# Issuing the q, k and v loads of a local-attention and feed-forward kernel from GpSimd instead of SyncE

## The chip, the cores and the metric

The kernel runs on one core of one Trainium2 chip. The metric is the device time of one execution in microseconds (us). A core has five engines with an instruction queue each: TensorE (PE, matrix products, with a weight load of its own, PEld), VectorE (DVE), ScalarE (ACT), GpSimd (POOL) and SyncE (SP), which here only issues transfers. Every engine takes its instructions in order, and a transfer (DMA) is an instruction in the queue of the engine that issues it: it waits there until its inputs and its buffer are ready, and what stands behind it waits too. The profile counts the transfers that GpSimd issues as one queue (q0, software_dynamic) and those that SyncE issues as another (q1, hardware_dynamic); both are carried out by the same 16 DMA engines.

## The reference

Local attention in chunks of 64 tokens, then a feed-forward layer with a leaky rectifier, all in float32:

```python
# q, k, v: (8 batches, 8 heads, 576 tokens, 64), cut to chunks of 64 tokens
scores = matmul(q_c, k_c.T) / 8 - max
attn   = exp(scores) / (sum(exp(scores)) + 1e-9)
out    = matmul(attn, v_c)                  # (4608 tokens, 512)
h      = out @ w_in                         # 512 -> 2048
result = (max(h, 0) + alpha * min(h, 0)) @ w_out   # 2048 -> 512
```

## The kernel before

The 4608 tokens are 36 sub-blocks of 128 tokens (two chunks, eight heads) and 9 blocks of 512 tokens. The first three blocks go through the feed-forward layer plainly: each of its products is done as three products of float32r halves (high by high, high by low, low by high). The other six blocks go in three pairs, with products of combined quarters (seven in place of eight); the quarters of the weights are computed in the first part on VectorE (`combine`, L607), written to DRAM by GpSimd (`keep_a`, L591) and streamed back through a ring of four buffers of 512 KB (`stream`, L643, issued by GpSimd too, L654).

The attention of the first eight sub-blocks is at the start, in an order written out by hand. Each of the other 28 (numbers 8 to 35) has a *visit* between two stretches of feed-forward products: 14 visits in the plain part, 14 in the first products of the first two pairs. At the visit of sub-block s (`visit_scores`, L512) TensorE does the value product of sub-block s-2 (L388) and the scores of s (L272). Then the loads of q and k of sub-block s+2 and of v of sub-block s are traced (`attn_load`, L232). A load has to wait for its buffer: q and k for the scores just done (two buffers each), v for the value product just done. The softmax of s follows on VectorE and ScalarE; VectorE transposes its result in blocks of 32 by 32 (L331), and eight transfers of 32 KB each (`attn_blocks`, L338) put the blocks in their places in the tile `pT`, from which the value product of s two visits later reads. So each visit has eleven transfers: three loads of 256 KB and eight of `pT`.

Other transfers that matter below: two sums of block 0 and 1 with an earlier part in DRAM are added by GpSimd's transfers (`partial<-g`, L499, and L636); the buffer `g` that the first of them reads is also the one that ScalarE fills with the negative part of the next hidden block (L406), which VectorE completes (L409). The results that were summed in DRAM are copied to the output by SyncE near the end of the plain part (`finals`, L957).

A planner orders each engine's queue from a simulated time line and from priorities; visits have a high priority. TensorE is kept in the order of tracing from the 21st step on. `tc.issue_after(ins)` puts instructions behind `ins` in its engine's queue. The hand-written start is not touched.

Of the kernel before, what the change touches and what calls it, by code (L numbers as in the profile page):

```python
# [59 lines left out]
def tile_local_attention_prelu_ffn(  # L60
# [12 lines left out]
    nc = tc.nc  # L73
    P = 128
    NSUB, C = qT.shape[1], 64
# [14 lines left out]
    EARLY = 2 * SPB  # L90
# [20 lines left out]
    def f32(t):  # L111
        return t.bitcast(F32)
# [103 lines left out]
    def prepare(f, behind=None):  # L216
        with tc.issue_after(behind.ins) if behind else nullcontext():
            for side in ("wi", "wo"):
                fetch(side, f)
                for _ in piece(side, f):  # L220
                    pass
# [2 lines left out]
    att = []  # L224

    qkv = {}
    loads = []
    probs = {}
    stages = {}
    pdiag = {}  # L230

    def attn_load(s, parts="qkv"):  # L232
        if "q" in parts:
            q_sb, kb = (load.tile([P, H, C], F32, name=name, bufs=2) for name in ("q_sb", "k_sb"))
            for t, src in ((q_sb, qT), (kb, kT)):
                nc.sync.dma_start(out=t, in_=src[:, s].rearrange("p (h t) -> p h t", t=C))
            qkv[s] = [q_sb, kb, None]
        if "v" in parts:
            v_sb = load.tile([P, DM], F32, name="v_sb", bufs=2)
            loads.append(nc.sync.dma_start(out=v_sb, in_=v[:, s]))  # L240
            qkv[s][2] = v_sb

    def banks_of(token):
# [83 lines left out]
    def attn_blocks(s):  # L327

        pr = probs.pop(s)
        tb = stage.tile([P, 2, H, HALF], F32, name="t3", bufs=2)  # L330
        nc.vector.transpose(tb.rearrange("p j h t -> p h j t"), pr)  # L331
        pT = load.tile([P, 2, H, HALF], F32, name="pT", bufs=2)
        for c in range(2):
            for i in range(2):
                for j in range(2):
                    src = slice(c * C + i * HALF, c * C + (i + 1) * HALF)
                    dst = slice(c * C + j * HALF, c * C + (j + 1) * HALF)
                    nc.sync.dma_start(  # L338
                        out=pT[dst, i].rearrange("p h t -> p (h t)"),
                        in_=tb[src, j].rearrange("p h t -> p (h t)"),  # L340
                    )
        pdiag[s] = pT
# [161 lines left out]
    def new_x():  # L504
        return (xp.tile([P, NK, TB], F32R, name="xh"), xp.tile([P, NK, TB], F32R, name="xl"))
# [22 lines left out]
    def visit_results(old, xo, new, sc3):  # L528
        if old is not None:
            attn_x(old, xo)  # L530
        if new is not None:
            attn_blocks(new)

    def visit(old, new):
        with tc.high_priority(offset=HIGH):
            parts = visit_scores(old, new)
            visit_softmax(*parts)
            visit_results(*parts)
# [9 lines left out]
    def first_v(s):  # L548

        v_sb = (vs + vs2)[s // 2].rearrange("p s h t -> p s (h t)")  # L550
        loads.append(nc.sync.dma_start(out=v_sb, in_=v[:, s:s + 2]))
        for i in range(2):
            qkv.setdefault(s + i, [None] * 3)[2] = v_sb[:, i]

# [42 lines left out]
    def keep_quarters(f):  # L597

        j, second = f % JF, f >= JF
        keep_a("wi", 4 if second else 1, j, wi[f][:, :, halves[second]])  # L600
        keep_a("wo", 4 if second else 1, j, wo[f][:, :, halves[second]])
        if second:
            keep_a("wo", 2, j, wo[f][:, :, halves[0]])
        else:
            keep_a("wi", 2, j, wi[f][:, :, halves[1]])

    def combine(side, j, early):  # L607

        ws = wi if side == "wi" else wo
        pair = [ws[j], ws[JF + j]]  # L610
        left, right = halves
        a = []
        for w, name in zip(pair, ("ta", "tb")):
            t = stage.tile([P, 512], F32, name=name, bufs=1)
            nc.vector.tensor_tensor(t, f32(w[:, 0]), f32(w[:, 1]), op=ALU.add)
            a.append(t)
        a11, a22 = a[0][:, left], a[1][:, right]
        if side == "wi":
            a12, a21 = a[0][:, right], a[1][:, left]
        else:  # L620
            a21, a12 = a[0][:, right], a[1][:, left]
        nc.vector.tensor_tensor(a22, a21, a22, op=ALU.add)
        nc.vector.tensor_tensor(a21, a11, a21, op=ALU.subtract)
        nc.vector.tensor_tensor(a11, a22, a11, op=ALU.subtract)
        nc.vector.tensor_tensor(a12, a12, a11, op=ALU.subtract)
        names = ((2, 4), (3, 1)) if side == "wi" else ((2, 3), (4, 1))
        for t, name, which in zip(a, names, ("raw", "raw" if early else "more")):
            w = scratch(which, [P, 2, 512], F32R)
            nc.scalar.copy(w[:, 0], t)
            nc.vector.tensor_tensor(w[:, 1], t, f32(w[:, 0]), op=ALU.subtract)  # L630
            for half, s in zip((left, right), name):
                stored = keep_a(side, {1: 5, 2: 6, 3: 7, 4: 3}[s], j, w[:, :, half])
            if adds:
                to, what = adds.pop(0)
                with tc.issue_after(stored.ins):
                    nc.gpsimd.dma_start(out=to, in_=what, accum_op=ALU.add)  # L636
# [231 lines left out]
    def new_raw(b):  # L868
        for n, name in enumerate(("xh", "xl")):
            x[b + n] = xp.tile([P, NK, TB], F32, name=name)  # L870
# [67 lines left out]
    for n, (p, b, f) in enumerate(steps):  # L938
        _, f0, f1 = phases[p]
        if f == f0:  # L940
            acc = accs[b] if p == 1 else []
            if p >= 3 and b + 1 < PLAIN:
                x[b + 1] = new_x()
        if n == 2 * NF:
            new_raw(PLAIN)
        if n == n0 + 1:

            tick = nc.gpsimd.tensor_copy(out=table, in_=f32(x[1][1])[:, 0, TB - 1:])
        if n0 < n <= n0 + NF:
            with tc.issue_after(tick.ins):  # L950
                keep_quarters(n - n0 - 1)
        pinned[0] = n >= 20
        if n == len(steps) - 1:
            with tc.issue_after(loads[-1].ins):
                while finals:
                    dst, src = finals.pop(0)
                    nc.sync.dma_start(out=dst, in_=src)  # L957
        if n < begun:
            continue
        if 2 * n in late:  # L960
            if 2 * n == visits[0]:
                with tc.issue_after(listed.ins):
                    for ahead in range(2):
                        attn_load(EARLY + ahead, "q")
            visit(*late[2 * n])
            parts, entry = held
            with tc.high_priority(offset=HIGH), tc.issue_after(stages["softmax"][0].ins):
                with tc.issue_after(stages["stored"].ins):
                    *_, entry[1] = parts
        if ready < NF:  # L970
            for ready in range(ready, min(n + 2, NF)):
                prepare(ready, split_ends.get(("wo", ready - 1)) if n == begun else None)
            ready += 1
        elif n in COMBINE:

            with tc.issue_after(stages["softmax"][0].ins), tc.issue_after(stages["softmax"][1].ins):
                combine(*combined.pop(0), n in (29, 35))
        if n == len(steps) - 8:
            ops, conversion = convert(PLAIN)
        if len(steps) - 8 <= n < len(steps) - 4:  # L980
            conversion.pop(0)()
        parts = first_layer(x[b], f)
        next(parts)
        entry = [acc, None, f, f0, f1, b, False]
        pending.append(entry)
        waits = 2 * n + 2 in late and n + 1 < len(steps)
        with tc.high_priority(offset=HIGH):
            next(parts)
            if not waits:
                next(parts)  # L990
        if 2 * n + 1 in late:
            visit(*late[2 * n + 1])
        if waits:
            held = parts, entry
        else:
            with tc.high_priority(offset=HIGH), (
                tc.issue_after(stages["softmax"][0].ins) if 2 * n + 1 in late else nullcontext()
            ):
                *_, entry[1] = parts
        if n >= len(steps) - 3:  # L1000

            with tc.issue_after(stages["split"][0].ins):
                for _ in range(3):
                    conversion.pop(0)()

        if len(pending) > (1 if n < 20 else 2):
            second(*pending.pop(0))
# [68 lines left out]
```

## Time and profile before

| | |
|---|---|
| median of 3 runs | 773.77 us (773.28 to 774.55) |
| the profiled execution's own time | 774.44 us |
| its span, first to last instruction | 772.6 us |
| TensorE busy | 760.5 us, 98% |
| VectorE, ScalarE, GpSimd busy | 84%, 58%, 24% |
| granted TensorE clock | 1.00 of full speed throughout |

Times inside the span are counted from its first instruction. The plain part lasts to about 304 us, the first pair to 464, the second to 621, the third to the end. Busy TensorE is not by itself TensorE at its peak; between large products the starts of neighbouring matrix products of 512 columns are 0.22 us apart where nothing holds them up.

### The profile page before, as it was taken

To read this page: it belongs to the slowest core of one execution; us is meant where nothing else is said; L and a number is where in the kernel's file an instruction comes from. 1 tells how busy PE (TensorE), PEld (TensorE's weight loads), DVE (VectorE), ACT (ScalarE), POOL (GpSimd) and SP (SyncE) were. 2 spreads that over 40 slices of the span, in tenths; PEclk is the share of its full clock that TensorE was granted. 3 is DMA by queue.
4 is the path that set the end of the run, shared out by engine and by line. 5 is a ranking of instruction groups with operands and counts; after the bars stand their busy time and mean duration, and the time that the engine had idled before them with its cause. 6 is when DMAs were issued, how large, how long until landed. Compare 5 with 4: busy or idle time off the path is not lost.

```text
span 772.6 us, 15413 instructions
## 1 busy us (share of the span) xinstructions
PE 760.5 (98%) x5558; PEld 639.8 (83%) x5558; DVE 647.7 (84%) x1140; ACT 448.2 (58%) x1221; POOL 184.8 (24%) x304
## 2 busy tenths in 40 slices
PE   7999999999999999999999999999999999999998
PEld 6788888878888888888888888888888888888886
DVE  6999989997979976877899898777898977679784
ACT  6975555566665674665756446654574544354642
POOL 1153322442525320111112111111121122112110
PEclk9999999999999999999999999999999999999999
DMA  9859496566969685888775678876556776655674
GB/s 359 325 194 385 175 329 210 174 237 179 285 206 260 231 302 168 293 283 273 258 246 200 229 248 280 273 236 209 204 203 219 253 233 193 202 205 193 199 242 158
DMA packets 69322, 184.52 MB, mean 239 GB/s; under 512 B 10992, under 2 KB 18176, under 8 KB 69120
## 3 DMA queue, kind: packets, MB, share of 16 engines
q0 software_dynamic: 34336, 119.56, 46.4%
q1 hardware_dynamic: 34480, 63.20, 24.2%
q8 instruction: 44, 0.72, 0.4%
q10 hardware_dynamic: 432, 0.79, 0.3%
q14 instruction: 30, 0.25, 0.1%
HBM read 135.27 MB, written 42.99 MB: 231 GB/s over the span
## 4 chain that ended last, share of the span: by engine, by line
PE 77%; DMA 6%; DVE 5%; ACT 5%; SPq 5%; issue 1%; POOL 0%; DVEq 0%; ACTq 0%
PE ps_o L717 19%; PE ps_o L845 19%; PE ps_h L717 10%; PE ps_h L845 10%; PE ps_h L421 7%; SPq L338 4%; PE ps_oa L457 4%; PE ps_ob L457 4%; DMA raw<-w_in 2%; DMA pT<-t 2%; PE ps_a L388 2%; ACT wi L313 1%; PE ps_a L272 1%; ACT wo L313 1%; DMA partial<-g 1%
## 5 line engine op out<-in xcount | busy, mean ns | idle before, releaser
L421 PE MATMUL ps_h<-xh,wi 128*128 128x512 f32 x384 | 101.7, 385 | 0.7 <-DVE g L409 0.5
L421 PEld LDWEIGHTS ps_h<-xh,wi 128*128 128x128 f32 x384 | 70.8, 187 | 13.8 <-PE ps_ob L457 0.8
L717 PE MATMUL ps_o<-wi,raw 128*128 128x512 f32 x336 | 79.1, 382 | 0.0
L717 PEld LDWEIGHTS ps_o<-wi,raw 128*128 128x128 f32 x336 | 62.5, 187 | 11.2
L673 ACT CAST gh<-wo 128x512 fp32r<-128x512 f32 x66 | 41.0, 621 | 47.3 <-PE ps_o L845 31.7
L287 ACT ACTIVATE pr<-ps_a,mx 128x64 f32<-128x64 f32 x224 | 67.4, 326 | 0.8
L457 PE MATMUL ps_oa<-wo,gh 128*128 128x512 f32 x192 | 58.4, 384 | 0.0
L457 PE MATMUL ps_ob<-wo,gh 128*128 128x512 f32 x192 | 57.7, 380 | 0.0
L421 PE MATMUL ps_h<-xl,wi 128*128 128x512 f32 x192 | 50.6, 381 | 0.0
L674 DVE TENSOR_TENSOR gl<-wo,gh 128x512 fp32r<-128x512 f32 x63 | 43.3, 687 | 7.5 <-ACT gh L673 7.1
L287 ACT ACTIVATION_READ_ACCUMULATOR pr<-ps_a,mx 128x1 f32 x224 | 48.7, 217 | 0.0
L654 POOL DMA_DIRECT2D raw<-wi_a x42 | 22.4, 533 | 96.1 <-PE ps_o L717 54.1
L654 POOL DMA_DIRECT2D raw<-wo_a x42 | 22.3, 531 | 90.7 <-PE ps_o L845 50.9
L406 ACT ACTIVATE wo<-gh 128x512 f32<-128x512 f32 x24 | 15.2, 633 | 48.4 <-DVE gh L747 48.4
L673 ACT CAST ta<-wo 128x512 fp32r<-128x512 f32 x42 | 26.1, 621 | 26.6 <-PE ps_o L845 15.5
L421 PEld LDWEIGHTS ps_h<-xl,wi 128*128 128x128 f32 x192 | 35.8, 187 | 6.8 <-DVE xl L375 0.3
L457 PEld LDWEIGHTS ps_ob<-wo,gh 128*128 128x128 f32 x192 | 35.9, 187 | 6.4
L457 PEld LDWEIGHTS ps_oa<-wo,gh 128*128 128x128 f32 x192 | 35.4, 187 | 6.6 <-DVE xl L375 0.2
L717 PE MATMUL ps_o<-wi,wo 128*128 128x512 f32 x168 | 40.4, 383 | 0.0
L717 PE MATMUL ps_o<-wi,wi 128*128 128x512 f32 x168 | 40.4, 383 | 0.0
L717 PE MATMUL ps_h<-wi,raw 128*128 128x512 f32 x168 | 40.4, 382 | 0.0
L435 ACT CAST gh<-g 128x512 fp32r<-128x512 f32 x48 | 30.2, 630 | 16.9 <-DVE g L409 15.0
(296 smaller groups left out, 2036.1 us busy)
## 6 DMA issues: line engine op xcount, KB each, us to landing
raw<-wi_a POOLq DMA_DIRECT2D x42, 512.0 KB, 4.5
raw<-wo_a POOLq DMA_DIRECT2D x42, 512.0 KB, 4.4
wi<-wi_a POOLq DMA_DIRECT2D x21, 512.0 KB, 4.4
wo<-wi_a POOLq DMA_DIRECT2D x21, 512.0 KB, 4.6
wi<-wo_a POOLq DMA_DIRECT2D x21, 512.0 KB, 4.2
wo<-wo_a POOLq DMA_DIRECT2D x21, 512.0 KB, 4.4
k_sb<-kT SPq DMA_DIRECT2D x28, 256.0 KB, 4.2
q_sb<-qT SPq DMA_DIRECT2D x28, 256.0 KB, 3.9
```

The lines of the kernel that those rows point to most:

```text
L287: last = nc.scalar.activation(pr[:, g], sc3[:, g // NP, g % NP], AF.Exp, bias=mx[:, g], scale=SCALE, accum_out=sm[:, g])
L313: last = nc.scalar.activation(pr[:, g], sc3[:, g % 2, g // 2], AF.Exp, bias=mx[:, g], scale=SCALE, accum_out=sm[:, g])
L338: nc.sync.dma_start(out=pT[dst, i].rearrange("p h t -> p (h t)"), in_=tb[src, j].rearrange("p h t -> p (h t)"),)
L388: pe(nc.tensor.matmul(att[0][par * C:(par + 1) * C, c, hp * C:(hp + 1) * C], lhsT=v_sb[rows, h * C:(h + 1) * C], rhs=p[rows, :, par * NP + ...
L421: pe(nc.tensor.matmul(woven(hps), lhsT=wi[f][:, l, k * P:(k + 1) * P], rhs=woven(xx[:, k]), start=(i == 0 and k == 0), stop=(i == 2 and k ...
L435: nc.scalar.copy(gh, g)
L457: pe(nc.tensor.matmul(woven(o), lhsT=a[:, ts], rhs=woven(wo[f][:, l]), start=(f == first and i == 0), stop=(f == last and i == 2),))
L654: streamed[0] = nc.gpsimd.dma_start(out=f32(t), in_=units[side][n])
L673: hi = nc.scalar.copy(t_hi, t)
L674: return hi, nc.vector.tensor_tensor(t_lo, t, f32(t_hi), op=ALU.subtract)
L717: pe(nc.tensor.matmul(woven(ps), lhsT=w[:, l, k * P:(k + 1) * P], rhs=woven(xx[:, xl]), start=first and at == 0, stop=at == n - 1, skip_gr ...
L845: pe(nc.tensor.matmul(woven(ps[m]), lhsT=w[:, l, m * P:(m + 1) * P], rhs=woven(xx), start=i in (1, 5, 2) and j == 0 and n == 0, stop=j == ...
```

## The change

The loads of sub-blocks 8 and 9 stay on SyncE; from sub-block 10 on (26 sub-blocks, 78 loads) they are issued by GpSimd. SyncE keeps the `pT` transfers and the stores. The `finals`, which were put behind the latest load of v, are put behind the latest `pT` transfer, since both must be on SyncE.

```diff
-    loads = []
     def attn_load(s, parts="qkv"):
+        queue = nc.sync if s < EARLY + 2 else nc.gpsimd
         if "q" in parts:
             ...
             for t, src in ((q_sb, qT), (kb, kT)):
-                nc.sync.dma_start(out=t, in_=src[:, s].rearrange("p (h t) -> p h t", t=C))
+                queue.dma_start(out=t, in_=src[:, s].rearrange("p (h t) -> p h t", t=C))
         if "v" in parts:
             v_sb = load.tile([P, DM], F32, name="v_sb", bufs=2)
-            loads.append(nc.sync.dma_start(out=v_sb, in_=v[:, s]))
+            queue.dma_start(out=v_sb, in_=v[:, s])
...
-                    nc.sync.dma_start(
+                    stages["blocks"] = nc.sync.dma_start(
                         out=pT[dst, i].rearrange("p h t -> p (h t)"),
...
-        loads.append(nc.sync.dma_start(out=v_sb, in_=v[:, s:s + 2]))
+        nc.sync.dma_start(out=v_sb, in_=v[:, s:s + 2])
...
-            with tc.issue_after(loads[-1].ins):
+            with tc.issue_after(stages["blocks"].ins):
```

## Rows read from the trace of the kernel before

**Rows 1.** The page, part 1: busy time and share of the span, instructions.
```profile
PE 760.5 (98%) x5558; PEld 639.8 (83%) x5558; DVE 647.7 (84%) x1140; ACT 448.2 (58%) x1221; POOL 184.8 (24%) x304
```

**Rows 2.** Busy time by stretch: length; busy (instructions) by engine; clock, DMA share, GB/s.
```profile
150.00:200.00 50.00, 49.25 (x455) 40.83 (x454) 44.99 (x91) 33.12 (x122) 17.49 (x23) 1.00 0.71 213
200.00:250.00 50.00, 49.15 (x512) 40.84 (x512) 44.05 (x86) 29.38 (x105) 22.25 (x29) 1.00 0.84 248
...
700.00:750.00 50.00, 50.00 (x229) 42.49 (x228) 40.76 (x66) 25.31 (x44) 10.10 (x19) 1.00 0.66 212
```

**Rows 3.** Waits of PE: line and releaser; total us, times, longest.
```profile
PE ps_a L388 <- DMA pT<-t: 1.1, 3, 0.4
```

**Rows 4.** PE in order of time, at visits: start us, us, instruction, count, idle before.
```profile
159.67 0.69 PE L388 MATMUL ps_a<-pT,v_sb 64*64 64x64 f32 x32
...
160.76 1.17 PE L421 MATMUL ps_h<-xh,wi 128*128 128x512 f32 x4
...
181.51 0.33 PE L388 MATMUL ps_a<-pT,v_sb 64*64 64x64 f32 x2
...
183.22 0.71 PE L457 MATMUL ps_oa<-wo,gh 128*128 128x512 f32 x2
...
191.35 0.69 PE L388 MATMUL ps_a<-pT,v_sb 64*64 64x64 f32 x32
...
212.45 0.33 PE L388 MATMUL ps_a<-pT,v_sb 64*64 64x64 f32 x2
...
214.28 0.71 PE L457 MATMUL ps_oa<-wo,gh 128*128 128x512 f32 x2
```

**Rows 5.** SP's queue in order of time.
```profile
173.97 5.68 SPq L338 DMA_DIRECT2D pT<-t  x8
...
183.47 5.64 SPq L338 DMA_DIRECT2D pT<-t  x8
...
199.61 0.53 SPq L236 DMA_DIRECT2D q_sb<-qT  x1
...
201.18 7.87 SPq L338 DMA_DIRECT2D pT<-t  x8
...
221.97 4.95 SPq L338 DMA_DIRECT2D pT<-t  x8
```

**Rows 6.** DVE in order of time.
```profile
182.08 0.75 DVE L409 SCALAR_TENSOR_TENSOR g<-g,rise,ps_h 128x512 f32<-128x512 f32 x1 [1.90 <-ACT g L406]
182.74 0.70 DVE L331 STREAM_TRANSPOSE t<-pr 128x512 f32<-128x512 f32 x1
...
199.85 0.70 DVE L331 STREAM_TRANSPOSE t<-pr 128x512 f32<-128x512 f32 x1
```

**Rows 7.** POOL in order of time, plain part.
```profile
174.47 1.45 POOL L593 DMA_DIRECT2D wi_a<-raw  x2
175.92 0.98 POOL L499 DMA_DIRECT2D partial<-g  x1
191.58 1.47 POOL L593 DMA_DIRECT2D wi_a<-raw  x2 [14.67 <-DVE raw L630]
```

**Rows 8.** ACT in order of time, around the wait for that sum.
```profile
174.64 0.62 ACT L491 COPY g<-ps_ob 128x512 f32<-128x512 f32 x1
...
181.45 0.60 ACT L406 ACTIVATE g<-ps_h 128x512 f32<-128x512 f32 x1 [2.56 <-DMA partial<-g]
```

**Rows 9.** Line L957, the finals: duration ns min/median/max, first and last start.
```profile
L957 SPq DMA_DIRECT2D out<-partial x8: 533/539/560, 284.8 to 294.3; - x8
```

**Rows 10.** POOL in order of time, first pair: streams.
```profile
326.70 0.53 POOL L654 DMA_DIRECT2D wi<-wi_a  x1 [2.11 <-PE ps_h L717]
...
335.93 0.53 POOL L654 DMA_DIRECT2D raw<-wi_a  x1 [2.11 <-PE ps_o L717]
```

**Rows 11.** Line L654, the streams: duration of an issue (ns), and time to landing.
```profile
L654 POOL DMA_DIRECT2D raw<-wi_a x42: 531/531/572, 274.0 to 679.7; - x42
...
DMA to landing us min/median/max: 3.4/4.5/6.5
```

## The prediction

> **What bounds the kernel now.** I read the page's busy times first. TensorE is busy for 98% of the span [rows 1], so whatever the change does, it shows only where it makes TensorE stand or lets it go on. Busy is not peak, so I next read TensorE's stretches and the starts of its products. Between 250 and 750 us each of the ten stretches of 50 us is busy to within 0.02 us, the last of them shown, and the large products start 0.22 us apart throughout. Idle time away from the two ends lies in two stretches: 0.75 us in 150 to 200 and 0.85 us in 200 to 250 [rows 2]. The granted clock is 1.00 in all of them, the upper of its two levels, and nothing in the change bears on it. The waits name the cause for most of it: the value product of a visit waits for transposed blocks, 1.1 us in three places [rows 3].
>
> What such a wait costs is more than its idle time. An undisturbed visit takes 160.76 - 159.67 = 1.09 us from its first small product to the next large one. The visit at 181.51 took 1.71, so it lost 0.62; the one at 212.45 took 1.83 and lost 0.74 [rows 4]. The third in the list I count like the second, which makes about 2.1 us in all. That is the most the change can give back: 0.27%. A difference of up to 0.2% (1.55 us) is what a measurement of this kernel can hardly tell from none, so only a nearly complete cure would be seen. There is much more room on the other side.
>
> **What leaves SyncE.** 78 of its issues. Per visit the three loads held SP's queue from 199.61 to 201.18, 1.57 us [rows 5]. Whether that matters depends on what stands behind. For the visit at 212.45 it does: the transposes on VectorE ended at 199.85 + 0.70 = 200.55, the `pT` group could begin only at 201.18 [rows 5, 6]. Beginning at once gives 0.63 us of the 0.74 lost; I take the part beyond the queue's usual lag of 0.05 us: **-0.58 us**. For the visit at 181.51 SP was free when the group began at 173.97, and the group took 5.68 us; TensorE needed its last piece 7.5 us after its start [rows 4, 5]. An earlier free SP gives nothing there. So one of the three waits is bought, and bounds for this part are 0 (the group is slow for another reason and stays so) and -2.1 us (all three go).
>
> Why groups differ in length (4.95 to 7.87 us) is not shown. If loads ahead in the same queue slow them, the change cures it. The group at 221.97 was the fastest, 4.95 us, although SP had issued three loads just before it; GpSimd was issuing nothing then. I take no change in length.
>
> **What the finals' new place costs.** The eight copies to the output were issued from 284.8 to 294.3 us [rows 9]; now all go behind the last `pT` group of the plain part, a few us later. Nothing reads them, and more than 470 us of the kernel follow: nothing. Were that cover gone, it would be their own delay.
>
> **What GpSimd takes on.** An issue of a stream takes 0.531 us, hardly ever more [rows 11]; a load has as many runs, half as long, so three cost about 1.59 us of GpSimd per visit, at most 3 x 0.73 = 2.2 us if they cost as much as the stores of quarters [rows 7]. GpSimd is busy for 24%, so its time is no bound; its order is. Three places count.
>
> First, loads behind a store that waits for VectorE. GpSimd stood still for 14.67 us until 191.58 [rows 7]. A load is traced at one visit and read two visits later, about 20 us (172 to 191, 191 to 212) [rows 4]; minus a landing of about 4.5 us this leaves 14 us or so. The planner places by readiness, and loads of the visits at 172 and 181 are ready long before that store, so they should stand ahead of it: nothing. If they stood behind, it would cost about 7 us.
>
> Second, stores behind loads, and one of them is tight. The sum `partial<-g` was issued at 175.92, and its input had been copied at 174.64 + 0.62 = 175.26; ScalarE then waited 2.56 us for it to land, and VectorE 1.90 us for ScalarE [rows 6 to 8]. VectorE's next instruction, at 182.74, is the transpose from which the group at 183.47 is fed [rows 5, 6]. That group ran to 189.11, and TensorE needed it at 191.35 without waiting [rows 4, 5]: 2.24 us from last issue to use, near the time such a transfer needs. The loads of the visit at 172.3 to 173.4 are ready two microseconds before the sum's input, and they have the higher priority. GpSimd has no gap there, stores standing end to end up to 175.92, so three issues ahead of the sum move it by 1.59 us, and with it ScalarE, VectorE, the group and TensorE. Bounds: 0, if the planner finds another order on VectorE or the loads stand behind; and 1.59 us plus the time in which 0.79 MB of loads pass through the same queue first. At the 248 GB/s of that part [rows 2] these are 3.2 us, so 4.8 us. Since the loads only add to four stores already queued and the rate is an average with pauses, I stay near the lower term: 1.59 minus half a microsecond of slack at 191.35, **+1.1 us**.
>
> Third, streams behind loads in the two pairs with visits. GpSimd issues a stream when TensorE gives a buffer back, 2.11 + 0.53 = 2.64 us apart [rows 10]. A buffer given back is read again after three others, 7.92 us later; a stream lands in 4.5 us, at most 6.5, so the slack is 3.4 us, at worst 1.4 [rows 11]. A visit separates give-backs by 1.09 us more, and three loads ready at its end fit before the next. If they delay one by a few tenths, the slack swallows it: nothing.
>
> The Trainium skill (DMA: Bandwidth & Descriptors, section "Issuing engines are not separate DMA queues") has it that transfers of all issuing engines interleave on the same 16 DMA engines and that a second issuing engine saves only the issuer's time, usually small. The trace agrees as far as GpSimd's streams and SP's loads overlap in it. By that rule alone the change is worth the 0.58 us above and no more.
>
> **Sum.** -0.58 + 1.1 = +0.5 us on the profiled execution's own 774.44 us (its span of 772.6 and 1.8 us around it), 774.96. The median of the runs lies 0.67 us below that execution, so the forecast is **774.3 us**, no change that can be told.
>
> **Rivals.** *Blocks freed.* Loads in front of the blocks in one queue are what slows the groups, and all waits of [rows 3] vanish, with the sum not delayed: 773.77 - 2.1 = 771.7. For it: the longest group comes straight behind loads [rows 5]. Against it: the fastest one too, and the loads still use the same engines. Chance 0.20.
>
> *The sum lands late.* The order of the second place holds and the loads' data pass before it: +4.8 - 0.5 of slack - 0.58 = +3.7, 777.5. It decides from a delay of about 2.6 us on, where the total leaves 0.2%. For it: ScalarE already stood for this landing, so there is no slack at its start. Against it: the planner sees the delay and may put the transpose ahead of L409. Chance 0.22. This one is slower.
>
> *A stream misses its turn.* In the pairs GpSimd holds a load that waits for the end of a visit in front of a stream whose buffer came free at its start: 1.09 + 1.59 = 2.7 us. It decides where the landing is slow (6.5 us, slack 1.4): 1.3 us of standing, at perhaps half of the 14 visits, 9 us in all, 783. Against it: the planner sees the give-back come first. Chance 0.07.
>
> *VectorE shuts GpSimd out.* If VectorE's work keeps GpSimd from writing its transfers' descriptors, each load takes longer; at the 0.98 us of the sum's issue [rows 7] it is 3 x 0.45 = 1.35 us more in the second place, 775.6. Against it: with VectorE busy for 84%, a stream's issue varies only from 0.531 to 0.572 us [rows 1, 11]. Chance 0.04, within the slower or the equal cases by halves. The Trainium skill (SBUF — State Buffer, section "SBUF: two separate sides") warns of that lock for transfers issued by GpSimd, 620 ns becoming 3100; by an estimate from that page three loads would hold GpSimd for 9.3 us. No row here shows it.
>
> **How the numbers follow.** The forecast has the remaining chance, 0.47, with its own range from -0.6 us (nothing of the second place) to +1.5 us, 773.2 to 775.3. Faster is the first rival, 0.20; slower the second, the third and half of the fourth, 0.31; the rest, 0.49, is the same. The range of 8 in 10 reaches from 771.6, the first rival whole, to 777.5, the second whole; left out are the lost streams and accidents of the planner on either side.
>
> **What would show it.** In the profile after, SP's queue should hold `pT` groups without loads between them, each beginning 0.1 us after its transposes, and the visit that now stands at 212.45 should take 1.09 us. GpSimd should show three loads of about 0.53 us after each visit, before the streams' next issue, and no idle TensorE between 304 and 620 us. `partial<-g` should be issued about 1.6 us later, ScalarE's L406 wait about 4 us, and the visit near 191 should wait for its blocks. I am wrong if the groups become short everywhere, if the loads stand behind a store that waits for VectorE, or if the planner deals VectorE's work out anew so that other waits appear.

## The result: 1.1% slower

| | before | after |
|---|---|---|
| median of the runs that were compared | 773.58 us (772.39 to 775.09, 6 runs) | 782.71 us (780.40 to 785.03, 6 runs) |
| span of the profiled execution | 772.6 us | 781.1 us |

The ratio is 1.0112, with a 95% interval of 1.0097 to 1.0128. The forecast of 774.3 us, and its range up to 777.5, were too low.

### The profile page after: what moved, and what is told of

Read it like the earlier page. It is cut to its first block, busy times and chain, and to the rows that moved or that the text cites. A ratio compares the mean times of both kernels' runs of the same rounds, so it can differ in the third digit from the quotient of the medians.

```text
span 781.1 us, 15438 instructions
## 1 busy us (share of the span) xinstructions
PE 764.5 (98%) x5558; PEld 643.3 (82%) x5558; DVE 647.5 (83%) x1140; ACT 448.1 (57%) x1221; POOL 226.8 (29%) x382
## 3 DMA queue, kind: packets, MB, share of 16 engines
q0 software_dynamic: 40576, 140.02, 54.3%
q1 hardware_dynamic: 23248, 42.75, 15.6%
## 4 chain that ended last, share of the span: by engine, by line
PE 82%; DMA 6%; DVE 5%; ACT 4%; SPq 2%; issue 1%; ACTq 0%; DVEq 0%
PE ps_o L717 19%; PE ps_o L845 19%; PE ps_h L421 10%; PE ps_h L717 10%; PE ps_h L845 9%; PE ps_oa L457 5%; PE ps_ob L457 5%; PE ps_a L388 2%; DMA pT<-t 2%; SPq L338 2%; DMA wo<-qT 2%; PE ps_a L272 2%; DMA raw<-w_in 1%; DMA raw<-w_out 1%; ACT pr L287 1%
## 5 line engine op out<-in xcount | busy, mean ns | idle before, releaser
L654 POOL DMA_DIRECT2D raw<-wo_a x42 | 22.2, 529 | 87.5 <-PE ps_o L845 50.4
L654 POOL DMA_DIRECT2D raw<-wi_a x42 | 22.4, 532 | 85.1 <-PE ps_o L717 50.8
L406 ACT ACTIVATE g<-ps_h 128x512 f32<-128x512 f32 x48 | 29.4, 612 | 19.2 <-PE ps_h L421 15.5
```

Source lines behind the costliest of these rows:

```text
L406: nc.scalar.activation(g, h, AF.Relu, scale=-1.0)
L654: streamed[0] = nc.gpsimd.dma_start(out=f32(t), in_=units[side][n])
```

## The profile after

Part 1 of the page, which answers to [rows 1]: TensorE's busy time and its share are 4 us and nothing apart from before, GpSimd has 42 us more.

```profile
PE 764.5 (98%) x5558; PEld 643.3 (82%) x5558; DVE 647.5 (83%) x1140; ACT 448.1 (57%) x1221; POOL 226.8 (29%) x382
```

Busy time by stretch, as in [rows 2]. The columns are the stretch, its length, each engine's busy time with its instructions, the granted clock, the DMA share and GB/s:

```profile
150.00:200.00 50.00, 47.47 (x447) 39.35 (x446) 43.03 (x87) 32.23 (x121) 24.54 (x37) 1.00 0.71 210
200.00:250.00 50.00, 46.83 (x479) 38.91 (x481) 40.51 (x80) 28.40 (x102) 25.93 (x37) 0.97 0.78 221
250.00:300.00 50.00, 48.00 (x418) 40.22 (x410) 41.99 (x81) 29.59 (x104) 22.17 (x34) 0.97 0.77 247
300.00:450.00 150.00, 150.00 (x1148) 126.21 (x1147) 122.17 (x208) 90.34 (x261) 38.86 (x73) 1.00 0.74 244
```

The loss lies in the plain part: TensorE is idle for 2.5, 3.2 and 2.0 us there, and in two of the stretches the granted clock is 0.97. In the pairs it is never idle: 150.00 of 150 us from 300 on, and the same from 450 to 600. The list of TensorE's waits names the cause, in the row that was [rows 3] before (total, times, longest):

```profile
PE ps_a L388 <- DMA pT<-t: 7.5, 3, 3.2
```

It is the same wait in the same number of places, though not all at the same visits, and 6.4 us longer. TensorE in order of time shows all three, and one visit without a wait:

```profile
181.08 0.33 PE L388 MATMUL ps_a<-pT,v_sb 64*64 64x64 f32 x2
183.76 0.63 PE L388 MATMUL ps_a<-pT,v_sb 64*64 64x64 f32 x27 [2.35 <-DMA pT<-t]
...
184.85 0.71 PE L457 MATMUL ps_oa<-wo,gh 128*128 128x512 f32 x2
...
214.08 0.69 PE L388 MATMUL ps_a<-pT,v_sb 64*64 64x64 f32 x32
...
215.17 0.71 PE L457 MATMUL ps_oa<-wo,gh 128*128 128x512 f32 x2
...
223.31 0.32 PE L388 MATMUL ps_a<-pT,v_sb 64*64 64x64 f32 x2
226.80 1.02 PE L388 MATMUL ps_a<-pT,v_sb 64*64 64x64 f32 x27 [3.17 <-DMA pT<-t]
...
228.71 1.53 PE L421 MATMUL ps_h<-xh,wi 128*128 128x512 f32 x3
...
258.70 0.33 PE L388 MATMUL ps_a<-pT,v_sb 64*64 64x64 f32 x2
260.96 1.02 PE L388 MATMUL ps_a<-pT,v_sb 64*64 64x64 f32 x27 [1.93 <-DMA pT<-t]
...
262.87 1.51 PE L421 MATMUL ps_h<-xh,wi 128*128 128x512 f32 x3
```

The visit at 214.08 takes the undisturbed 1.09 us. The three others take 3.77, 5.40 and 4.17 us to the next large product, so they lose 2.68, 4.31 and 3.08. Behind the second and third the next large products are slow too, as the chain of waits shows (start, length, what):

```profile
178.60 5.03 DMA pT<-t
...
206.00 2.87 PE ps_h L421 x12
...
220.18 6.48 DMA pT<-t
...
228.78 3.47 PE ps_h L421 x12
...
255.16 5.66 DMA pT<-t
...
262.94 3.45 PE ps_h L421 x12
```

Twelve large products took 2.87 us behind an undisturbed visit, 3.47 and 3.45 behind these two: 0.60 and 0.58 us more. The sum is 2.68 + 4.31 + 3.08 + 1.18 = 11.25 us. The waits of before cost some 2.1 by the prediction's count, which leaves 9.15; the profiled execution was 0.43 us ahead of before at the first of these visits (181.08 against 181.51 [rows 4]), which makes 8.7. The spans differ by 8.5 us.

Why the blocks land late is seen at the visit at 181. The first lines here are from before, the second from after, both for the `pT` group that begins near 174 us: issues with duration in ns (min, median, max) and first and last start, then the time from issue to landing in us (min, median, max).

```profile
L338 SPq DMA_DIRECT2D pT<-t x8: 513/592/1250, 174.0 to 179.1; - x8
DMA to landing us min/median/max: 2.7/3.7/4.8
```

```profile
L338 SPq DMA_DIRECT2D pT<-t x8: 507/594/1228, 173.6 to 178.6; - x8
DMA to landing us min/median/max: 3.5/5.0/5.4
```

After the change SyncE issued the last block 0.5 us *earlier*, issues took as long as before, and yet the blocks landed later: 5.0 us from issue against 3.7. Nor did the group begin late for the visit that needs it: from its first issue to the first small product of that visit there are 7.5 us before (173.97 to 181.51 [rows 4, 5]) and 7.5 after (173.6 to 181.08). Only the time from the first issue to the last landing grew, from 7.9 to 10.1 us. What runs at that time is seen on GpSimd, after the change (start, length, instruction):

```profile
175.47 0.98 POOL L499 DMA_DIRECT2D partial<-g  x1
176.07 0.97 POOL L240 DMA_DIRECT2D v_sb<-v  x1
176.63 0.95 POOL L236 DMA_DIRECT2D q_sb<-qT  x1
177.16 0.95 POOL L236 DMA_DIRECT2D k_sb<-kT  x1
```

Three loads of 256 KB go out in the middle of the group. Before, SyncE issued them behind the group, for the group held its queue. The other two late groups have the same picture: loads from 217.57 in the group whose last issue is at 220.18, and from 252.53 in the one whose last issue is at 255.16, with landing medians of 5.7 and 5.8 us. The first of the two:

```profile
L338 SPq DMA_DIRECT2D pT<-t x8: 507/596/1299, 215.1 to 220.2; - x8
...
DMA to landing us min/median/max: 3.5/5.7/6.5
```

That the loads' data is what delays the blocks is so far an inference from times that coincide; the experiments test it.

## The experiments

Three theories were stated. A: the loads' data run through the DMA engines beside the blocks, and so the blocks land late. B: the order in GpSimd's queue, where stores now stand behind loads, makes VectorE and the transposes late; or the issues on GpSimd cost by themselves. C: GpSimd's queue is served ahead of SyncE's. Ratios are against the kernel before on the same chip; its median was 773.83 us beside e1 to e4, 774.67 beside e5 to e8 and 774.52 beside e9 to e11.

**Finals only.** The kernel after, with all loads back on SyncE:

```diff
-        queue = nc.sync if s < EARLY + 2 else nc.gpsimd
+        queue = nc.sync
```

> All loads go back to SyncE; only the new place of the copies to the output, behind the last group of transposed blocks, is left. Both theories: nothing reads these copies, so no change, 773.6 us within 1.5. If it comes out above 776, part of the loss is here.

Measured: 773.65 us, ratio 0.9998 (0.9988 to 1.0007). The finals' new place costs nothing.

**Only q and k, and only v.** The kernel after with v's loads (e2), or those of q and k (e3), on SyncE:

```diff
-            queue.dma_start(out=v_sb, in_=v[:, s])
+            nc.sync.dma_start(out=v_sb, in_=v[:, s])
```

> GpSimd issues the loads of q and k (0.52 MB a visit), SyncE those of v. Theory A (the loads' data now run through the DMA engines beside the eight transfers of the blocks, whose landing is late, 5 to 6.5 us): the delay goes with the bytes that run beside them, so about two thirds of the 9 us, 779 to 780 us, with waits of the value products for blocks of some 5 us. Theory B (the order of GpSimd's queue: stores of quarters and sums stand behind loads, so VectorE and its transposes are late): the loads that wait longest in GpSimd are those of v, so most of the loss goes with v and this one is near 775.

> GpSimd issues the loads of v alone (0.26 MB a visit). Theory A: about a third of the loss or less, 775 to 777 us, waits for blocks 2 to 3.5 us. Theory B: GpSimd still stands for the value products before each load of v, so most of the loss stays, 780 to 783.

Measured: 780.32 us, 1.0086 (1.0069 to 1.0104), with q and k on GpSimd; 776.07 us, 1.0025 (1.0016 to 1.0034), with v there. TensorE's waits for `pT` are 4.9 and 1.6 us in all. This speaks against theory B, which put most of the loss on v's loads (near 775 without them on GpSimd, 780 to 783 with them alone). Theory A came near: 0.3 us above its interval with q and k, inside it with v, whose waits are less than the 2 us it asked for. Two loads cost more than twice what one does; whether q's or k's weighs more isn't parted.

**Loads held back on GpSimd until the blocks have landed.** From the kernel after; a copy of two columns of the latest `pT`, on GpSimd, stands ahead of the loads of the plain part:

```diff
-    small.tile([P, 24], F32, name="rest")
+    rest = small.tile([P, 24], F32, name="rest")
...
+    def gate(new):
+        if new - 1 not in pdiag or not EARLY + 2 <= new < EARLY + len(visits):
+            return nullcontext()
+        landed = nc.gpsimd.tensor_copy(out=rest[:, :2], in_=pdiag[new - 1][:, :, 0, 0])
+        return tc.issue_after(landed.ins)
...
-            if new + 2 < NSUB:
-                attn_load(new + 2, "q")
-            attn_load(new, "v")
+            with gate(new):
+                if new + 2 < NSUB:
+                    attn_load(new + 2, "q")
+                attn_load(new, "v")
```

> All loads stay with GpSimd, but in the plain part they wait until the blocks of the sub-block before have landed (a copy of two columns of that tile on GpSimd, behind which the loads stand). Same queue, same bytes, some 8 us later. Theory A: the landings go back to 2 to 4 us, the waits for blocks fall below 2 us in all, 772 to 774 us. Theory B: GpSimd now stands longer in front of the stores, so it gets no better than 782, rather worse.

Measured: 780.89 us, 1.0089 (1.0074 to 1.0104). Its waits, TensorE's first and then one of GpSimd's:

```profile
PE ps_a L388 <- ACT xl L399: 1.9, 1, 1.9
PE ps_a L388 <- DMA pT<-t: 1.6, 3, 1.0
PE ps_h L421 <- DVE g L409: 1.4, 2, 1.3
...
POOL rest L515 <- DMA pT<-t: 39.4, 8, 7.1
```

With the loads behind the blocks, the waits for blocks fall from 7.5 to 1.6 us, as theory A has it. But GpSimd takes its instructions in order: it stood for 39.4 us at the gates, and what stood behind them came late (ScalarE's cast into `raw`, L636, waited 5.8 us for a store of `raw`; in the kernel before, where it is L629, 3.4). TensorE now stands for ScalarE and VectorE. So B's mechanism is possible in this kernel, but here it is the gate that brings it about. Theory A's time, 772 to 774 us, was missed by 7 us, and one group, from 214.2 us, still landed with a median of 5.7 us, beside loads that had passed the gate just before it. The time says nothing for either theory; the waits do.

**Loads on GpSimd in the pairs alone.**

```diff
-        queue = nc.sync if s < EARLY + 2 else nc.gpsimd
+        queue = nc.gpsimd if s >= (24 if "q" in parts else 22) else nc.sync
```

> GpSimd issues the loads only at the visits of the two pairs; the plain part has them on SyncE as before. Theory A (all of the loss is late blocks in the plain part): same as the kernel before within 1.5 us, 772.5 to 774.5, and no idle TensorE after 310 us. The rival of the prediction that streams miss their turn behind loads: 778 to 783.

Measured: 774.06 us, 0.9998 (0.9985 to 1.0010). All of the loss comes from the loads of the plain part. In the kernel after the blocks land later in the pairs too (a median of 4.4 us over the 112 issues there, before 3.8), but a group there has more room: the one that begins at 322.3 us is read at 334.9, 12.6 us later, where the first late group has 7.5.

**Loads on SyncE ahead of the blocks.** From the kernel after: the eight transfers of a group are held until the next visit's loads have been traced, and stand behind those in SyncE's queue.

```diff
-                    stages["blocks"] = nc.sync.dma_start(
-                        out=pT[dst, i].rearrange("p h t -> p (h t)"),
-                        in_=tb[src, j].rearrange("p h t -> p (h t)"),
-                    )
+                    moves.append((pT[dst, i].rearrange("p h t -> p (h t)"), tb[src, j].rearrange("p h t -> p (h t)")))
...
+    def move():
+        with ExitStack() as after:
+            while latest_loads:
+                after.enter_context(tc.issue_after(latest_loads.pop().ins))
+            while moves:
+                out, in_ = moves.pop(0)
+                stages["blocks"] = nc.sync.dma_start(out=out, in_=in_)
...
```

The finals, which nothing reads, stand behind the latest load of v again.

> All loads on SyncE, but ahead of the eight transfers of the blocks that are ready at the same time, so that they run through the DMA engines when GpSimd's loads did. Theory A (the time at which the loads run, whichever queue): at least as slow as the change, 781 to 786. Theory C (the loads do harm because GpSimd's queue is served before SyncE's): only the three issues in front count, 1.6 us at each of the tight visits, 775 to 779.

Measured: 812.24 us, 1.0487 (1.0465 to 1.0509). Waits of TensorE and of SyncE:

```profile
PE ps_a L399 <- DMA pT<-t: 22.1, 16, 2.8
...
SPq L243 <- PE ps_a L399: 100.2, 24, 6.8
```

This is far slower than expected, with TensorE idle in the pairs as well (busy for 141.46 of the 150 us from 300 on), and it can't be read for A: SyncE stood 100.2 us for the value products that give v's buffer back, with the blocks behind it in the queue. The run shows what SyncE's queue costs when loads that wait for a buffer stand in front. In the kernel before loads stood in front of a group too (at 201.18 [rows 5]), but did not wait there, and delayed it by the prediction's 0.63 us.

**Half of the blocks' transfers on GpSimd, or on ScalarE.** From the kernel before; GpSimd in e7, ScalarE in e8:

```diff
-                    nc.sync.dma_start(
+                    (nc.gpsimd if j else nc.sync).dma_start(
                         out=pT[dst, i].rearrange("p h t -> p (h t)"),
```

> The kernel before (loads on SyncE, behind the blocks), but four of each eight block transfers are issued by GpSimd. If the wait for blocks comes from eight issues in a row on one queue (5 us), the last piece lands some 2.5 us earlier and all waits for blocks go: 771 to 772. If GpSimd takes them late because of stores ahead of them, waits stay or grow: 774 to 778.

> The same with ScalarE as the second issuer. ScalarE has no long waits for VectorE's stores, but each issue takes its time from the softmax and the rectifier: 771 to 772 if an issue costs it under 0.1 us, 774 to 780 if it costs 0.5 us as on SyncE (2 us more per visit on an engine that VectorE waits for).

Measured: 774.73 us, 1.0002 (0.9992 to 1.0012), with GpSimd, and 792.02 us, 1.0233 (1.0212 to 1.0255), with ScalarE. With GpSimd the waits for `pT` fell from 1.1 to 0.6 us, but others came up (1.1 us for ScalarE's L491, 0.9 for its L399), so a shorter group bought nothing, and the 771 to 772 us of that reading were missed. On ScalarE each issue took 0.61 us of the queue of an engine that feeds the softmax and the hidden layer. The expected 774 to 780 us were missed by 12; TensorE's longest wait was 7.6 us, for which the profile names no releaser, so what makes this run so slow is open.

**Fewer bytes, the same instructions.** From the kernel after; a quarter of the bytes in e9, half in e10. The products take the two (four) heads that are fetched for all eight, so the other heads' part of the output is left out.

```diff
-                queue.dma_start(out=t, in_=src[:, s].rearrange("p (h t) -> p h t", t=C))
+                part = H if s < EARLY + 2 else H // 4
+                queue.dma_start(out=t[:, :part], in_=src[:, s, :part * C].rearrange("p (h t) -> p h t", t=C))
...
-            queue.dma_start(out=v_sb, in_=v[:, s])
+            part = DM if s < EARLY + 2 else DM // 4
+            queue.dma_start(out=v_sb[:, :part], in_=v[:, s, :part])
```

The control, e11, has the quarter too, but `queue = nc.sync` as in the kernel before.

> The changed kernel, its loads on GpSimd cut to a quarter of their bytes: from sub-block 10 on only the first two heads of q, k and v are fetched and their data stand for all eight heads, so the outputs of the other heads are left out. The number and order of instructions on every engine stay those of the changed kernel. Theory A (the loads' data run through the DMA engines beside the transposed blocks): 773 to 775.5 us, TensorE's waits for pT at or below 1.5 us in all, and the blocks' landing in the groups at 173, 215 and 250 us back from 5 to 6 us to some 4. Theory B (the order in GpSimd's queue, stores standing behind the loads) and any theory by which the mere issue on GpSimd costs: 780 to 783 us, as the changed kernel. Theory C (GpSimd's queue is served ahead of SyncE's): as A, since what is served ahead is bytes; this run doesn't part A from C.

> As the run with a quarter, with half of the bytes: four heads of q, k and v are fetched and stand for all eight; the other heads' outputs are left out. Theory A: between the two, 775 to 779 us, with waits for pT of 1.5 to 4.5 us. Theory B or a cost of the issues: 780 to 783 us.

> Control for the run with a quarter: the same quarter of the bytes (two heads for all eight, the others left out), but the loads stay on SyncE as in the kernel before. What it is faster than the kernel before is what fewer bytes are worth by themselves, whoever issues. Theory A: 772 to 774 us, since in the kernel before the loads run after the blocks and 1.1 us of waits for pT is all there is to win, and within 1.5 us of the quarter on GpSimd. Theory B or a cost of the issues: 772 to 774 us here too, but 7 to 9 us below the quarter on GpSimd.

Measured: a quarter on GpSimd 775.81 us, 1.0014 (1.0005 to 1.0024); half 777.94 us, 1.0038 (1.0025 to 1.0051); a quarter on SyncE 773.70 us, 0.9984 (0.9974 to 0.9994). GpSimd in the run with a quarter issues the same instructions in the same order, at almost the same times:

```profile
175.88 0.98 POOL L501 DMA_DIRECT2D partial<-g  x1
176.48 0.96 POOL L242 DMA_DIRECT2D v_sb<-v  x1
...
177.57 0.94 POOL L237 DMA_DIRECT2D k_sb<-kT  x1
```

TensorE's waits for `pT` are 2.0 us with a quarter, 4.1 with half and 0.2 in the control. And the landing of the quarter run's group from 214.3 to 220.3 us, where the kernel after had a median of 5.7 (in the groups at 174.0 and 246.3 us the medians are 4.0 and 2.9, where it had 5.0 and 5.8):

```profile
L340 SPq DMA_DIRECT2D pT<-t x8: 507/597/1452, 214.3 to 220.3; - x8
...
DMA to landing us min/median/max: 3.1/3.7/5.0
```

The issues stayed and the bytes went, and most of the loss went with them. That speaks against B and against a cost of the mere issues. In order of what GpSimd loads per visit, with the waits of the one profiled execution:

| KB per visit on GpSimd | run | ratio to before | waits for `pT`, us |
|---|---|---|---|
| 0 | finals only | 0.9998 | 1.1 |
| 192 | a quarter of each | 1.0014 | 2.0 |
| 256 | v | 1.0025 | 1.6 |
| 384 | half of each | 1.0038 | 4.1 |
| 512 | q and k | 1.0086 | 4.9 |
| 768 | the change | 1.0112 | 7.5 |

The time rises with the bytes, though the number of issues (three, one, three, two, three) does not. The steps at the small end are not certain: the intervals of 192 and 256 KB overlap, and their waits stand the other way round. Theory A's numbers were missed by a little: the quarter run came out 0.3 us above its interval with 2.0 us of waits in place of 1.5, and 2.1 us above its control, where 1.5 was the limit. That remainder may be the quarter of the data that still runs beside the blocks, or the issues themselves; it isn't parted here. Three quarters of the bytes are worth 7.6 us on GpSimd (1.0112 less 1.0014, of 774 us) and 1.2 us on SyncE (1 less 0.9984), so 6.4 of the change's 8.7 us are shown to come from bytes that GpSimd loads at the time it does. Nor is C parted from A: bytes that are served first and bytes that share equally would both give this table.

One more thing changed with the queue, and no run here parts it. Part 3 of the profile's page counts 34480 packets and 63.20 MB in SyncE's queue before and 23248 and 42.75 after; in GpSimd's 34336 and 119.56 before and 40576 and 140.02 after. So each of the 78 loads went as 144 packets from SyncE, but as 80 larger ones from GpSimd. In the run with a quarter the packets fell with the bytes, to 32 a load, so the table would look the same if it is the packets that hold the blocks up.

The Trainium skill (DMA: Bandwidth & Descriptors, section "Queues, rings and completion order") says that each DMA engine takes turns between the queues it has work for, a packet from one and then from the next. The landings agree with a share that is taken by the other queue; the order of the turns no run here shows.

## Why the prediction was wrong

**The step that failed** is the one about the blocks under "What leaves SyncE": "If loads ahead in the same queue slow them, the change cures it. [...] I take no change in length." Length was taken as the time of SyncE's issues. That did not change in the group at 174 (5.1 us from first to last issue before, 5.0 after), and in the long one at 201.18 it even fell, from 6.9 to 5.1 us. The time from issue to landing was never a term of the sum, and it went from a median of 3.7 to 5.0 us in the group at 174. The bounds of that part, 0 and -2.1 us, had no loss in them. The sentence just before held the clue: the fastest group, at 221.97 in the kernel before, ran while "GpSimd was issuing nothing". This is its landing in the trace of before, and what the two queues moved from 221.9 to 227 us (packets, MB, share); behind it the landing of the group at 201.18:

```profile
L338 SPq DMA_DIRECT2D pT<-t x8: 512/589/590, 222.0 to 226.3; - x8
DMA to landing us min/median/max: 1.8/2.6/3.9
...
q1 hardware_dynamic: 727, 0.99, 58.3%
q0 software_dynamic: 33, 0.04, 4.7%
...
L338 SPq DMA_DIRECT2D pT<-t x8: 512/882/1878, 201.2 to 208.1; - x8
...
DMA to landing us min/median/max: 4.4/5.0/6.6
```

In these groups the landing goes with what GpSimd has out. Blocks land in a median of 1.9 us in the group at 183.47, where GpSimd moves nothing, and in 2.6 here, although three loads of SyncE's own queue are in flight just ahead of them (0.99 MB, of which the blocks are 0.26). They take 3.7 us at 173.97 beside four of GpSimd's stores and a sum, and 5.0 at 201.18, beside eight stores and a sum and no load of GpSimd's. After the change the three late groups, with three loads on top of the stores, take 5.0 to 5.8 us. So far as these groups show, loads are not special; they join what GpSimd already has out, at the three visits with the least room. In the old order they went between one group and the next in SyncE's queue and never into the middle of one; the prediction priced the queue as 1.57 us of lost time per visit and not as the order that it also was.

**The loads' time on SyncE, -0.58 us.** The visit that stood at 212.45 now takes 1.09 us, as forecast (it begins at 214.08). Its group begins at 202.25, 11.83 us before it, where it was 11.27, so the gain is 0.56 us. It is too small to be told in the whole.

**The sum behind the loads, +1.1 us.** Wrong too, but as a loss that did not come: the planner put the loads behind `partial<-g`, which was issued at 175.47 and not later than before (175.92 [rows 7]). ScalarE, in order of time, waited hardly longer than the 2.56 us of [rows 8], and TensorE had no wait at the visit that followed:

```profile
181.32 0.60 ACT L406 ACTIVATE g<-ps_h 128x512 f32<-128x512 f32 x1 [2.89 <-DMA partial<-g]
```

That order was right for the sum, and put the loads into the middle of the group instead.

**Loads behind a store that waits for VectorE, nothing.** Right: the loads of the visit at 181 were issued from 184.76, and the store came behind them at 191.71.

**The finals, nothing.** Right (e1). They now run from 296.2 us, where [rows 9] had 284.8.

**Streams behind loads, nothing.** Right (e5). The first pair on GpSimd, which answers to [rows 10], has three loads between two streams and still a pause of 0.36 us before the next:

```profile
323.41 0.53 POOL L654 DMA_DIRECT2D wi<-wi_a  x1 [1.89 <-PE ps_h L717]
325.39 0.54 POOL L240 DMA_DIRECT2D v_sb<-v  x1 [1.45 <-PE ps_a L388]
...
326.45 0.54 POOL L236 DMA_DIRECT2D k_sb<-kT  x1
327.35 0.53 POOL L654 DMA_DIRECT2D wo<-wi_a  x1 [0.36 <-PE ps_o L717]
```

**The rivals.** *Blocks freed* had the sign of the effect wrong; its own counter-argument, "the loads still use the same engines", points at the cause. *The sum lands late* did weigh the loads' data, at 3.2 us, but only for a transfer in the same queue. Nothing weighed it for transfers of the other queue. *VectorE shuts GpSimd out* did not happen: in the pairs a load took 0.54 us, and in the plain part, where some of the loads lasted longer (0.95 us and more), their issues still began 0.53 to 0.57 us apart.

**The rule that was weighed.** The Trainium skill (DMA: Bandwidth & Descriptors, section "Issuing engines are not separate DMA queues") was read as "the change is worth the 0.58 us above and no more". The trace agrees with its first half, that transfers of all issuers interleave on the same engines: SyncE's blocks took 5.0 us to land beside GpSimd's loads, and 3.7 without them. It is that half which costs here: issuing earlier from another engine made transfers run together that had run one after the other.

**The clock.** That "nothing in the change bears on it" was wrong as well: see below.

## What to carry to other kernels

Before you move a transfer to a free queue, ask what its old queue made it wait for. In this kernel the loads that stood behind a group of blocks in one queue left it the DMA engines until it was issued; let out early, with some 10 us to spare, they slowed the transfers that TensorE was about to need. So give a moved transfer a landing time beside what now runs with it, and price the change in the landing of the urgent transfer, not only in issue time.

## What the hardware showed that was not expected

The lower clock stands behind part of the loss. Busy time by stretch, after the change, around the longest wait (3.17 us, until 226.80):

```profile
223.00:227.00 4.00, 0.83 (x12) 0.42 (x14) 0.54 (x1) 0.60 (x1) 0.00 (x0) 0.94 0.67 168
227.00:236.00 9.00, 9.00 (x92) 7.76 (x89) 7.10 (x15) 5.82 (x23) 1.69 (x4) 0.83 0.34 104
236.00:245.00 9.00, 9.00 (x100) 7.47 (x100) 7.76 (x15) 3.20 (x13) 7.81 (x11) 1.00 0.88 224
```

TensorE stood idle, then the granted clock was at the lower of its two levels (1.2 GHz) for part of the next stretch, 0.83 in the mean, and at the upper again afterwards. In that time 27 small products took 1.02 us where they took 0.63 at 183.76. The wait of 1.93 us until 260.96 was followed by the same 1.02, the one of 2.35 us until 183.76 was not. So the length of the wait alone doesn't tell, in these rows, whether the clock falls.

The size of the effect on landing was not expected either: with 768 KB of loads issued beside it, the group from 215.1 us landed with a median of 5.7 us, while the mean DMA share of the stretch from 200 to 250 us was 0.78, lower than the 0.84 of before [rows 2]. A mean share below 1 does not mean that a transfer lands undisturbed.
